# Batch 0's prologue: the third q pair transposed ahead of the second, the copies in that order, one dummy matmul taken out

## The chip, the cores and the metric

The kernel runs on one core of one Trainium2 chip. The metric is the device time of one execution in microseconds (us), as a median over runs. A profiled execution has its own span, counted from the first instruction of the program; it is some 2 us shorter than the timed value. The engines are PE (TensorE; "PEld" is its weight load), DVE (VectorE), ACT (ScalarE), POOL (GpSimd) and SP, which only issues DMAs here.

## The reference, cut to what matters

```python
q_s = softmax(q, axis=-1)            # 8 batches, 8 heads, 576 rows, 64 columns
k_s = softmax(k, axis=2)
kv  = einsum('bhsd,bhse->bhde', k_s, v)
x   = einsum('bhsd,bhde->bhse', q_s, kv)      # then to (4608, 512)
h   = x @ w_in                                # (512, 2048)
out = (h * sigmoid(beta * h)) @ w_out         # (2048, 512)
```

Nearly all the work is in the two products at the end. The attention of batch 0 is the prologue: nothing of the large products can start before it.

## The kernel before

Heads go in four pairs per batch. For each pair of batch 0, q is exponentiated (ACT), summed and scaled (DVE or POOL), transposed by PE into PSUM, and copied to SBUF. For each pair, PE also forms kv from exp(k) and v, and DVE scales the result. A matmul of the two gives x.

```python
def tpe(b, j, tag):          # four 128x128 transposes of pair j (PE)
    ...
def q_ev(b, j, eng):         # copy of the transposed pair to SBUF
    evac(eng, qsT[b][:, :, j, :], tp_of.pop((b, j))[:])
def kvz_mm(b, j, ...):       # kv group j: 18 small matmuls from exp(k) and the cast v
    ...
def kvz_norm(b, j, ...):     # DVE: one reciprocal, two multiplies
    ...
def warm(n, tag):            # n dummy matmuls 128x128x512 on zeros
    ...
```

The order written in the program is the order on each engine. The stretch around the change, and what comes a little later:

```python
q_mul(0, 2, 4, eng=G)        # pair 2 scaled on POOL
kz_exp(0, 0)
q_mul(0, 1, 4)               # pair 1 scaled on DVE
warm(10, tag="acc2")
beta_pe("acc0")
tpe(0, 3, "acc1")
tpe(0, 1, "acc2")
q_ev(0, 3, V)
tpe(0, 2, "acc3")
kz_exp(0, 1)
beta_ev()
q_ev(0, 1, V)
q_ev(0, 2, V)
vz_cast(0, 0, G)             # v of pair 0 cast on POOL
warm(1, tag="b0")
kz_exp(0, 2)
kvz_mm(0, 0, "b3", 1)
# ... three more kv groups, x of the four pairs, h(0,0) to h(0,3) ...
hpe(0, 7, [0], "b2")         # first product, block of columns 7, quarter 0 of w_in
th_act(0, 2)
hpe(0, 7, [1])
hpe(0, 4, [2])               # needs quarter 2 of w_in block 1
# ... then the second product of batch 0, mm_b(0, 0) to mm_b(0, 11) ...
kvz_mm(1, 0, "b1", 1)        # kv group of batch 1's first pair
tpe(1, 3, "b3")
```

The softmax here doesn't subtract the row's maximum and nothing guards it: scores larger than these inputs give would overflow.

Of the kernel before, what the change touches and what calls it, by code (L numbers as in the profile page):

```python
# [17 lines left out]
def kernel(  # L18
# [151 lines left out]
    def evac(eng, dst, src):  # L170
        if eng is nc.scalar:
            eng.copy(dst, src)  # L172
        else:
            eng.tensor_copy(dst, src)  # L174
# [8 lines left out]
    def kz_exp(b, j):  # L183
        if j == 0:
            ek_buf(b)
        nc.scalar.activation(ek[b][:, j, :], k_st[b][:, j, :], ACTF.Exp)  # L186
# [28 lines left out]
    def vz_cast(b, j, eng, m=1, part=None):  # L215
        r = slice(0, RW) if part is None else (slice(0, 5), slice(5, RW))[part]
        evac(
            eng,
            va[b][:, j : j + m, r, 0:D],
            v_st[b][:, j : j + m, :].rearrange("p j (i d) -> p j i d", i=RW)[:, :, r, :],  # L220
        )
# [63 lines left out]
    def bank(tag):  # L285
        if tag not in turns:
            return tag
        turns[tag] += 1
        return (HB if tag == "h" else AB)[(turns[tag] - 1) % 2]
# [3 lines left out]
    def tpe(b, j, tag):  # L293
        if j == 0:
            qsT[b] = work.tile([P, R, HP, P], BF16, tag="qsT", bufs=2, name=f"qsT{b}")
        tp_of[b, j] = ps.tile([P, R, P], BF16, tag=bank(tag), bufs=1, name=f"tp{b}_{j}")
        for i in range(R):
            nc.tensor.transpose(  # L298
                tp_of[b, j][:, i, :],
                eq[b][:].rearrange("p i (j x) d -> p i j (x d)", j=HP)[:, i, j, :],  # L300
                identity[:],
            )

    def q_ev(b, j, eng):
        evac(eng, qsT[b][:, :, j, :], tp_of.pop((b, j))[:])
# [222 lines left out]
    def warm(n, tag):  # L528
        t = ps.tile([P, 512], F32, tag=bank(tag), bufs=1, name=f"warm{warm_n[0]}")
        warm_n[0] += 1  # L530
        for _ in range(n):
            nc.tensor.matmul(t[:], xT[2][:, 0, 0:P], xT[2][:, 0, :])  # L532

    V, A, G = nc.vector, nc.scalar, nc.gpsimd
# [27 lines left out]
    def beta_pe(tag):  # L562
        tb = ps.tile([P, 512], F32, tag=bank(tag), bufs=1, name="tb")
        tb_of.append(tb)
        nc.tensor.transpose(tb[:, 0 : NJ // 2], beta_r[:, 0 : 2 * P : 2], ident8[:])
        nc.tensor.transpose(tb[:, NJ // 2 : NJ], beta_r[:, 1 : 2 * P : 2], ident8[:])

    def beta_ev():
        tb = tb_of[0]
        nc.scalar.copy(  # L570
            beta_t[:].rearrange("p (hh e) -> p e hh", e=2),
            tb[:, 0:NJ].rearrange("p (e hh) -> p e hh", e=2),
        )
# [62 lines left out]
    warm(10, tag="acc2")  # L636
    beta_pe("acc0")
    tpe(0, 3, "acc1")
    tpe(0, 1, "acc2")
    q_ev(0, 3, V)  # L640
    tpe(0, 2, "acc3")
    kz_exp(0, 1)
    beta_ev()
    q_ev(0, 1, V)
    q_ev(0, 2, V)
    vz_cast(0, 0, G)
    warm(1, tag="b0")
    kz_exp(0, 2)
    kvz_mm(0, 0, "b3", 1)
    vz_cast(0, 1, G)  # L650
# [340 lines left out]
```

## Time and profile before

| | value |
|---|---|
| time, median of the first three runs | 281.67 us (281.64 to 282.98) |
| profiled span | 279.8 us |
| PE busy | 272.2 us, 97% of the span |
| first kv matmul of batch 0 | 11.32 us |
| first reciprocal of the norms | 11.84 us |
| x of pair 2 | 13.94 us |
| h(0,4) with the late quarter of w_in (quarters 2 and 3 of block 1 come in one load) | 19.42 us |
| DMA rate from 9 to 36 us | 381 to 398 GB/s |

A PE that is busy 97% of the time tells that almost any saving elsewhere is hidden.

### The profile page before, as it was taken

The numbers are of one execution on the slowest core, as the hardware profiler recorded it, in microseconds if no ns is written. First come the engines' busy times: TensorE is split into PE (matmuls) and PEld (weight loads), VectorE is DVE, ScalarE is ACT, GpSimd is POOL, SyncE is SP. The second block draws the span as 40 slices with busy tenths as digits, with TensorE's granted clock in tenths as the row PEclk, the third lists the DMA queues.
The fourth block names the chain that finished last, engine by engine and source line by source line (L and its number), as shares of the span: only waits on it lengthen the run. The fifth ranks groups of instructions, "written<-read, shape, count | busy, mean of one in ns | idle before, by whom it ended". The sixth has DMA issues, their size and how long they took to land.

```text
span 279.8 us, 4448 instructions
## 1 busy us (share of the span) xinstructions
PE 272.2 (97%) x1712; PEld 128.0 (46%) x1739; DVE 174.9 (63%) x284; ACT 162.0 (58%) x247; POOL 40.5 (14%) x61
## 2 busy tenths in 40 slices
PE   8899999999999999999999999999999999999995
PEld 3444454444444444444444444444444544445444
DVE  3864786994478456944595549553864596354362
ACT  4757885947486447744684458444733574454451
POOL 1854227133030003000300021000000000000000
DMA  7999999999972991199318961641154034005004
GB/s 247 389 394 392 386 389 318 331 284 177 319 248 38 251 297 70 64 236 291 112 76 183 270 188 75 133 94 81 69 89 140 0 152 75 0 0 152 0 0 150
DMA packets 55316, 50.09 MB, mean 179 GB/s; under 512 B 26616, under 2 KB 47488, under 8 KB 55296
## 3 DMA queue, kind: packets, MB, share of 16 engines
q1 hardware_dynamic: 54368, 48.97, 60.2%
q10 hardware_dynamic: 928, 0.85, 0.9%
q8 instruction: 13, 0.21, 0.3%
q14 instruction: 7, 0.06, 0.1%
HBM read 36.71 MB, written 9.44 MB: 165 GB/s over the span
## 4 chain that ended last, share of the span: by engine, by line
PE 94%; DMA 3%; issue 1%; DVE 1%; ACT 1%; SPq 0%
PE h L404 45%; PE acc L453 43%; DMA k_st<-in_k_dram 3%; PE kv L342 2%; PE x L373 1%; PE acc L445 1%; PE kv L317 1%; PE x L389 1%; PE tp L298 1%; DVE kvp L332 0%; ACT ek L186 0%; DVE rk L329 0%; SPq L109 0%; ACT o L172 0%; PE x L364 0%
## 5 line engine op out<-in xcount | busy, mean ns | idle before, releaser
L418 DVE SCALAR_TENSOR_TENSOR g<-th,h 128x512 bf16<-128x512 bf16 x144 | 96.0, 681 | 79.4 <-ACT th L414 79.2
L414 ACT ACTIVATE th<-h,beta_t 128x512 bf16<-128x512 f32 x144 | 97.7, 686 | 81.9 <-PE h L404 81.3
L404 PE MATMUL h<-xT,w_in_b 128*128 128x512 bf16 x566 | 142.3, 379 | 0.8
L453 PE MATMUL acc<-w_out_b,g 128*128 128x512 bf16 x543 | 137.8, 379 | 1.5 <-issue 1.3
L404 PEld LDWEIGHTS <-w_in_b 128*128 128x128 bf16 x576 | 55.9, 98 | 66.3 <-ACT w_in_b L172 0.4
L453 PEld LDWEIGHTS <-g 128*128 128x128 bf16 x560 | 53.8, 98 | 66.0 <-issue 2.5
L174 POOL CAST va<-v_st 128x320 bf16<-128x320 f32 (+2 forms) x14 | 16.6, 1191 | 108.9 <-DMA v_st<-in_v_dram 108.9
L262 DVE TENSOR_REDUCE rq<-eq 128x16 f32<-128x1024 bf16 (+1 forms) x20 | 22.1, 1105 | 5.6 <-ACT eq L251 5.1
L268 DVE TENSOR_TENSOR eq<-eq,rq 128x1024 bf16<-128x1024 bf16 (+1 forms) x18 | 22.1, 1227 | 0.1
L172 ACT CAST xT<-x 128x512 bf16<-128x512 f32 x18 | 9.9, 588 | 17.0 <-PE x L373 14.9
L251 ACT ACTIVATE eq<-q_st 128x1024 bf16<-128x1024 f32 (+1 forms) x18 | 16.9, 955 | 3.4 <-DMA q_st<-in_q_dram 3.4
L174 DVE COPY o<-acc 128x512 f32<-128x512 f32 (+2 forms) x20 | 12.6, 641 | 3.6 <-PE acc L453 3.4
L172 ACT COPY o<-acc 128x512 f32<-128x512 f32 (+1 forms) x18 | 9.5, 570 | 8.5 <-PE acc L453 4.6
L174 DVE CAST xT<-x 128x512 bf16<-128x512 f32 x18 | 11.5, 682 | 2.6 <-PE x L373 1.8
L193 ACT ACTIVATE ek<-k_st 128x1024 bf16<-128x1024 f32 x12 | 12.6, 1050 | 0.0
L532 PE MATMUL warm<-xT 128*128 128x512 bf16 x25 | 8.0, 482 | 1.2 <-DVE xT L613 1.2
L174 POOL CAST w_in_b<-w_in 128x512 bf16<-128x512 f32 (+1 forms) x10 | 6.5, 656 | 5.7 <-DMA w_in<-in_moe_w_in_dram 5.5
L174 POOL CAST w_out_b<-w_out 128x1024 bf16<-128x1024 f32 x5 | 5.2, 1040 | 6.5 <-DMA w_out<-in_moe_w_out_dram 6.5
L186 ACT ACTIVATE ek<-k_st 128x576 bf16<-128x576 f32 x8 | 5.2, 679 | 1.0 <-DMA k_st<-in_k_dram 0.9
L263 DVE RECIPROCAL rq<-rq 128x16 f32<-128x16 f32 (+1 forms) x20 | 4.9, 243 | 0.7
L342 PEld LDWEIGHTS <-ek 128*64 128x64 bf16 x192 | 4.1, 111 | 2.5 <-issue 2.5
L532 PEld LDWEIGHTS <-xT 128*128 128x128 bf16 x25 | 2.9, 120 | 5.1 <-issue 2.8
(49 smaller groups left out, 84.7 us busy)
## 6 DMA issues: line engine op xcount, KB each, us to landing
out_dram<-o SPq DMA_DIRECT2D x14, 512.0 KB, 3.2
q_st<-in_q_dram SPq DMA_DIRECT2D x25, 256.0 KB, 4.1
k_st<-in_k_dram SPq DMA_DIRECT2D x6, 1024.0 KB, 9.6
v_st<-in_v_dram SPq DMA_DIRECT2D x6, 1024.0 KB, 11.1
w_in<-in_moe_w_in_dram SPq DMA_DIRECT2D x6, 512.0 KB, 9.9
v_st<-in_v_dram SPq DMA_DIRECT2D x8, 288.0 KB, 7.9
w_out<-in_moe_w_out_dram SPq DMA_DIRECT2D x4, 512.0 KB, 8.9
w_out<-in_moe_w_out_dram SPq DMA_DIRECT2D x2, 1024.0 KB, 10.5
```

The lines of the kernel that those rows point to most:

```text
L172: eng.copy(dst, src)
L174: eng.tensor_copy(dst, src)
L193: nc.scalar.activation(ek[b][:, :, h, :].rearrange("p i h d -> p h i d"), k_st[b][:, h, 0 : R * D].rearrange("p h (i d) -> p h i d", i=R), ...
L251: nc.scalar.activation(eq[b][:, :, s * m : (s + 1) * m, :].rearrange("p i h d -> p h i d"), q_st[b][:, s * m : (s + 1) * m, :].rearrange(" ...
L262: nc.vector.tensor_reduce(rq[b][:, 0, :, h], eq[b][:, :, h, :], axis=AX.X, op=ALU.add)
L268: eng.tensor_tensor(eq[b][:, :, h, :], eq[b][:, :, h, :], rq[b][:, 1, :, h].unsqueeze(3).to_broadcast((P, R, m, D)), ALU.mult,)
L342: nc.tensor.matmul(t[r * D : (r + 1) * D, j, :], ek[b][:, i, hd, :] if i < R else ekt[(b // 2) % 2][:, ds(hd * D, D)], va[b][:, i, hd, :] ...
L404: nc.tensor.matmul(h[:], w_unit(j, kt), x_of(c)[:, kt, :], start=(kt == 0), stop=(kt == KT - 1),)
L414: nc.scalar.activation(th[:], h_of[c, j][:], ACTF.Tanh, scale=beta_t[:, j : j + 1])
L418: nc.vector.scalar_tensor_tensor(out=g[:], in0=th_of.pop((c, j))[:], scalar=1.0, in1=h_of[c, j][:], op0=ALU.add, op1=ALU.mult)
L453: nc.tensor.matmul(acc[st][:], g[:, ds(st * P, P)], w_out_b[:, j, :], start=(j == 0), stop=(j == NJ - 1),)
L532: nc.tensor.matmul(t[:], xT[2][:, 0, 0:P], xT[2][:, 0, :])
```

## The change

Pair 2's scaled q is ready on POOL 0.55 us before pair 1's on DVE. The change lets PE transpose pair 2 first, in time in which it stood idle, makes DVE copy in the same order, and takes out the one dummy matmul ahead of the first kv group.

```diff
     beta_pe("acc0")
     tpe(0, 3, "acc1")
+    tpe(0, 2, "acc3")
+    q_ev(0, 3, V)
     tpe(0, 1, "acc2")
-    q_ev(0, 3, V)
-    tpe(0, 2, "acc3")
     kz_exp(0, 1)
     beta_ev()
+    q_ev(0, 2, V)
     q_ev(0, 1, V)
-    q_ev(0, 2, V)
     vz_cast(0, 0, G)
-    warm(1, tag="b0")
     kz_exp(0, 2)
     kvz_mm(0, 0, "b3", 1)
```

## The prediction

> **What bounds the kernel now.** I read the busy table of the page first, then the chain of waits over the first 15 us (the only stretch that the change touches), then each engine in order of time from 8.5 to 19.6 us, and last the waits of PE from 19.5 us on.
>
> ```profile
> PE 272.2 (97%) x1712; PEld 128.0 (46%) x1739; DVE 174.9 (63%) x284; ACT 162.0 (58%) x247; POOL 40.5 (14%) x61
> ```
>
> PE is busy 272.2 of 279.8 us, so the kernel is one long stream of matmuls and a change of order pays only where PE stands still. That is mostly in the prologue. The chain of waits, restricted to 9 to 12.2 us (start, length, what):
>
> ```profile
> 9.11 1.26 ACT ek L186 x2
> 10.37 0.07 ACT beta_t L570
> 10.44 0.13 issue
> 10.56 0.61 PE tp L298 x8
> 11.17 0.21 PE warm L532
> 11.39 0.43 PE kv L317 x18
> 11.81 0.02 issue
> 11.84 0.18 DVE rk L329
> ```
>
> The eight transposes (pairs 1 and 2), the dummy matmul and kv group 0 lie one after another on the path to the first reciprocal at 11.84. The wait before 10.56 is put down to the copy of beta. By the order of the program the first transpose of pair 1 cannot wait for that copy, which comes later; what it needs is pair 1's scaled q, and that multiply on DVE ends at the same moment (9.28 + 1.14 = 10.42). From 11.84 the chain is DVE alone: four norms of 0.69 us each (reciprocal plus two multiplies: rk at 11.84, 12.53, 13.22, 13.91), then x and the h matmuls. DVE and POOL in order of time:
>
> ```profile
> 9.28 1.14 DVE L268 TENSOR_TENSOR eq<-eq,rq 128x512 bf16<-128x512 bf16 x1
> 10.34 0.41 DVE L174 COPY qsT<-tp 128x512 bf16<-128x512 bf16 x1
> 10.99 0.75 DVE L174 COPY qsT<-tp 128x512 bf16<-128x512 bf16 x2 [0.23 <-PE tp L298]
> ...
> 8.82 1.05 POOL L268 TENSOR_TENSOR eq<-eq,rq 128x512 bf16<-128x512 bf16 x1
> 9.87 1.07 POOL L174 CAST va<-v_st 128x576 bf16<-128x576 f32 x1
> ```
>
> POOL finishes pair 2's scaled q at 9.87, 0.55 us ahead of pair 1's: today pair 1 is transposed first and pair 2 waits behind it. POOL then casts the first v group until 10.94, and kv group 0 cannot start before that.
>
> The decisive view is a few us later, everything in order of time from 18.6 to 19.6:
>
> ```profile
> 18.74 0.62 ACT L172 CAST w_in_b<-w_in 128x512 bf16<-128x512 f32 x1
> 18.77 0.61 POOL L174 CAST w_in_b<-w_in 128x512 bf16<-128x512 f32 x1 [1.40 <-DMA w_in<-in_moe_w_in_dram]
> 18.91 0.10 PEld L404 LDWEIGHTS <-w_in_b 128*128 128x128 bf16 x1 [0.28 <-issue]
> 19.27 0.68 ACT L414 ACTIVATE th<-h,beta_t 128x512 bf16<-128x512 f32 x1
> 19.41 0.11 PEld L404 LDWEIGHTS <-w_in_b 128*128 128x128 bf16 x2 [0.41 <-ACT w_in_b L172]
> ```
>
> POOL has been idle 1.40 us for the second half of w_in block 1 and starts when it lands, about 18.72; ACT casts its quarter in the same moment, until 19.36; the weight load of h(0,4) with that quarter starts at 19.41. So the matmul stream is pinned here by a landing, not by what came before. It hardly shows today: the matmul ahead starts at 19.12, 0.216 is one matmul, so PE would have gone on at 19.34 and loses only 0.08 us. From 19.5 to 39 the table of waits has no wait of PE: after 19.41 the order is simply worked off.
>
> **What the Trainium skill says.**
> - "TensorE: Matmul & The Clock Gate", Part 1: the array runs at half clock until it was busy about 3.4 us, and goes back after about that long an idle window. The trace agrees with the first: the dummies start 0.427 us apart until 5.43 and 0.216 us apart from then on. The longest gap of PE after that is 0.61 us, so taking the dummy away should not lower the clock.
> - The same page, Part 4, gives a PE transpose about 275 ns in a kernel. Here one takes 218 ns (median of 16) and starts follow each other by 0.055 us; I use these.
> - "GPSIMD Engine Reference", section 1, says that GpSimd shares its SBUF interfaces with VectorE, with contention when DVE has two SBUF inputs. The trace agrees: DVE's multiply beside POOL took 1.14 us against 0.69 alone, and the 128x576 cast 1.07 us in that overlap against 0.67 for the next.
> - "Perfetto Trace Analysis", Roofline, puts one core's ceiling at about 435 GB/s, that of its 16 DMA engines. Here DMA moves 387 to 398 GB/s from 9 to 36 us and the share of its engines is at 1.02 or above: the queue is full, and a landing time there follows from bytes, not from compute.
>
> **The change part by part.** The program after has two PE rows fewer (weight load and matmul of the dummy); the other engines have the same rows, DVE with copies 2 and 1 swapped. No DMA moves.
>
> (a) Pair 2's transposes first. PE ends pair 3's at about 9.96; pair 2 is scaled at 9.87, so its four go at about 10.0 and are done by 10.4, in what is idle time today. Pair 1's still start at 10.56 (DVE multiply) and end at 10.95. Four transposes x 0.055 = 0.22 us leave PE's path.
>
> (b) No dummy. The first kv matmul starts 0.31 us after the dummy's start (11.01 to 11.32). Without (a) the dummy costs about 0.2 us.
>
> (a) and (b) together would let kv group 0 start at about 10.9 (last transpose starts 10.73, plus some 0.15 by today's hand-overs). But the v cast ends at 10.94, so I take 11.00: **0.32 us** earlier than 11.32, not 0.42.
>
> (c) The copies. The copy of pair 3 stays at 10.34; copy 2 follows at 10.68 (back to back, 0.34 apart as today's last two), copy 1 at 11.02 to 11.43. kv group 0, 0.50 us from first start to last end, ends at 11.50; the reciprocal starts at about 11.53 instead of 11.84. DVE is free by then. **0.31 us** earlier.
>
> (d) The norms still take 0.69 us each, so the fourth starts at 13.60. kv groups 1, 2 and 3 wait for casts that do not move (ending 11.56, 11.95, 12.59), which lets group 3 end at about 13.2, still ahead of its norm. x of pair 2 goes at 13.62 instead of 13.94, and the h stream starts 0.31 us earlier. Its first weights, landing one after another and cast by 13.44, 14.10, 14.78 and 15.46, are there early enough.
>
> (e) At h(0,4)'s third matmul PE arrives at about 19.03 instead of 19.34 and waits until 19.41 all the same. The 0.08 us wait becomes about 0.39 us. **Sum at the end of the kernel: 0.31 won, 0.31 lost again, 0.0 us.**
>
> **The rivals.**
> 1. The gain survives: the w_in quarter could come earlier too. For it: an ACT that is 0.3 us ahead is free before the landing. Against: POOL, free for 1.40 us, could not start before 18.77 either, and the loads of that stretch are issued without waiting for anything that the change speeds up. If I am wrong here, 281.35 us (281.67 - 0.31).
> 2. The path is not shortened at all: the v cast or the contention of the earlier copies with POOL's casts holds kv group 0, or DVE's copies become the wait. For it: the cast ends only 0.38 us before today's kv start. Against: it is done at 10.94. The end would be the same 281.67, so the time cannot tell this from my theory; only the trace can.
> 3. Slower: without the dummy PE's clock falls back. A half-clock window of 3.4 us would cost some 1.7 us (estimate from the page on TensorE named above). Against: gaps of under 1 us, and the wait at 19.4 stays under 0.5 us. I give it a few per cent at most.
>
> **Range and chances.** The runs before are 281.64, 281.67 and 282.98. I predict **281.65 us**: no change, with a breath of the 0.08 us stall's jitter. The low end, 281.3, takes in rival 1; the high end, 282.1, takes in a median pushed by one of the longer executions. 2% would be 5.6 us, eighteen times all that is in play: faster 0.01, same 0.98, slower 0.01.
>
> **What the profile after would show.** Right: pair 2's transposes at about 10.0; first kv matmul near 11.0; first reciprocal near 11.5; x of pair 2 near 13.6; the POOL cast of w_in block 1 still at 18.77 with its long wait, and the weight load behind ACT's cast at 19.41 after a longer wait (about 0.3 us more in the matmul starts); from there the same times as before. Wrong: the load at 19.41 moved earlier (rival 1), the reciprocal still near 11.8 (rival 2), or matmuls 0.43 us apart after 9 us (rival 3). A shift of the landings themselves, which I take as fixed, would also break it.

## The result, and the profile after

The kernel after takes 281.93 us (median of six, 281.72 to 282.38), the kernel before 281.72 us in the runs set against it (281.61 to 282.98). The ratio is 1.0003, with a 95% interval of 0.9983 to 1.0022: the same. A ratio here is the mean of one kernel's fast runs over the mean of the other's in the same rounds, so it is not quite the ratio of the medians. The 0.2 us between the medians lie inside the interval, and nothing more is made of them. The interval is also too wide to choose between the prediction and its rival 1: 281.35 us would be 0.9987 of 281.72 and lies inside it. The choice rests on the traces.

First the prologue of the kernel after. DVE, POOL and PE in order of time from 9.3 to 12 us; the columns are start, length, engine, line and operation, output from input, and how many were merged:

```profile
9.43 1.15 DVE L268 TENSOR_TENSOR eq<-eq,rq 128x512 bf16<-128x512 bf16 x1
10.49 1.07 DVE L174 COPY qsT<-tp 128x512 bf16<-128x512 bf16 x3
11.66 0.17 DVE L329 RECIPROCAL rk<-kv 128x1 f32<-128x1 f32 x1
...
10.04 2.07 POOL L174 CAST va<-v_st 128x576 bf16<-128x576 f32 x3
...
9.70 1.32 PE L298 MATMUL tp<-identity,eq 128*128 128x128 bf16 x12
11.15 1.03 PE L317 MATMUL kv<-va,ek 64*64 64x65 bf16 x33
```

The page merges all twelve transposes in one row; their single records start at 9.70 us (pair 3), 10.08 us (pair 2) and 10.63 us (pair 1), so pair 2 now goes while DVE still scales pair 1. The three copies run back to back, and the first reciprocal is at 11.66 instead of 11.84. In this execution the loads landed about 0.14 us later than in the profile of before (k at 9.23 instead of 9.09 us), so against the landing of k the reciprocal is 0.32 us earlier: 11.659 - 9.230 = 2.43 us after it, where it was 11.836 - 9.089 = 2.75.

Then the place that the prediction called decisive. Everything in order of time from 18.6 to 19.7 us, the kernel after; the bracket gives the idle time ahead of an instruction and what ended it:

```profile
18.86 0.62 ACT L172 CAST w_in_b<-w_in 128x512 bf16<-128x512 f32 x1 [0.34 <-DMA w_in<-in_moe_w_in_dram]
18.89 0.62 POOL L174 CAST w_in_b<-w_in 128x512 bf16<-128x512 f32 x1 [1.36 <-DMA w_in<-in_moe_w_in_dram]
...
19.53 0.11 PEld L404 LDWEIGHTS <-w_in_b 128*128 128x128 bf16 x2 [0.70 <-ACT w_in_b L172]
19.53 0.39 PE L404 MATMUL h<-xT,w_in_b 128*128 128x512 bf16 x1 [0.21 <-ACT w_in_b L172]
```

ACT, which came straight from other work before, now waits 0.34 us for the landing as well, and PE for ACT's cast. The two matmuls on either side start 0.591 us apart. A matmul takes 0.216, so 0.375 us are lost, where it was 0.297 - 0.216 = 0.08. The chain of waits of the kernel after, from 9 us on, says it in another way:

```profile
2.65 8.08 DMA v_st<-in_v_dram
10.74 0.02 issue
10.75 8.08 DMA w_in<-in_moe_w_in_dram
18.83 0.02 issue
18.86 0.63 ACT w_in_b L172
19.48 0.04 issue
19.53 2.33 PE h L404 x10
```

In the kernel before this chain went through the prologue: exp of k, transposes, dummy, kv, norms, x. None of those is left in it. The prologue became shorter than the loads, and the path to the end now runs through the DMA: a load of v lands at 10.73 us, the second half of w_in block 1 is issued behind it at 10.75 and lands at 18.83.

A second place was not in the prediction. POOL and PE in order of time near 39 us, kernel before, then kernel after:

```profile
38.49 0.93 POOL L174 CAST va<-v_st 128x320 bf16<-128x320 f32 x1 [2.09 <-DMA v_st<-in_v_dram]
...
39.47 0.48 PE L317 MATMUL kv<-va,ek 64*64 64x65 bf16 x18
```

```profile
38.59 0.95 POOL L174 CAST va<-v_st 128x320 bf16<-128x320 f32 x1 [2.07 <-DMA v_st<-in_v_dram]
...
39.59 0.48 PE L317 MATMUL kv<-va,ek 64*64 64x65 bf16 x18
```

The kv group of batch 1's first pair starts 0.05 us after a cast of v that has itself waited over 2 us for its load. A full matmul and the first kv matmul behind it are at best 0.309 us apart in these traces; here it is 0.387 and 0.390, so each kernel waits 0.08 us. This is a second pin in the same stream (a place where the matmuls wait for a load), and both kernels end 240.34 to 240.36 us after it.

So the time can be cut into three stretches: from the landing of k to x of pair 2 (the prologue), from there to the kv group (1,0) (the stretch that waits for loads), and from there to the end. These are read from single records of the traces, and used below for all runs:

| run | k landed | prologue | to kv (1,0) | to the end |
|---|---|---|---|---|
| before | 9.09 | 4.85 | 25.54 | 240.36 |
| after | 9.23 | 4.53 | 25.83 | 240.34 |

The prologue is 0.32 us shorter and the next stretch 0.30 us longer.

The landing of k is not the best mark to measure from. What holds the prologue are the multiplies of pairs 1 and 2 and the cast of v behind one of them, and these follow q's second load, issued on ACT; k landed 3.01 to 3.04 us after it in ten of the 13 profiles, but 3.19 us in that of run 3. From the landing of that q load to x of pair 2 it is 7.88 to 7.89 us in all five profiles with the old order and the dummy (before and runs 5, 7, 9, 11) and 7.55 to 7.56 us in all six with the whole change (after and runs 3, 4, 6, 8, 10). So the 0.33 us are far above the scatter between executions.

### The profile page after: what moved, and what is told of

Same layout as the page of the kernel before. It is cut to its first block, busy times and chain, and to the rows that moved or that the text cites. A ratio compares the mean times of both kernels' runs of the same rounds, so it can differ in the third digit from the quotient of the medians.

```text
span 279.9 us, 4472 instructions
## 1 busy us (share of the span) xinstructions
PE 274.4 (98%) x1738; PEld 128.0 (46%) x1738; DVE 174.4 (62%) x284; ACT 162.1 (58%) x247; POOL 40.7 (15%) x61
## 4 chain that ended last, share of the span: by engine, by line
PE 92%; DMA 6%; SPq 1%; ACT 0%; issue 0%
PE acc L453 44%; PE h L404 43%; DMA v_st<-in_v_dram 3%; DMA w_in<-in_moe_w_in_dram 3%; PE kv L342 2%; PE x L373 1%; PE acc L445 1%; PE kv L317 1%; PE tp L298 0%; PE x L389 0%; ACT w_in_b L172 0%; SPq L578 0%; SPq L132 0%; SPq L109 0%; SPq L135 0%
## 5 line engine op out<-in xcount | busy, mean ns | idle before, releaser
L453 PE MATMUL acc<-w_out_b,g 128*128 128x512 bf16 x560 | 141.0, 379 | 0.0
L532 PE MATMUL warm<-xT 128*128 128x512 bf16 x24 | 7.3, 466 | 1.2 <-DVE xT L613 1.2
L354 DVE RECIPROCAL rk<-kv 128x4 f32<-128x4 f32 x6 | 1.1, 182 | 6.5 <-PE kv L342 6.5
```

The lines of the kernel that those rows point to most:

```text
L453: nc.tensor.matmul(acc[st][:], g[:, ds(st * P, P)], w_out_b[:, j, :], start=(j == 0), stop=(j == NJ - 1),)
L532: nc.tensor.matmul(t[:], xT[2][:, 0, 0:P], xT[2][:, 0, :])
```

## The experiments

The theory: the prologue's gain is real, and two late loads take it back, one at 19.4 us and one at 39.5 us. The rivals: the gain comes from another part of the change than thought; one load alone holds the kernel; an engine's queue between 20 and 39 us takes it; the landing could be moved. Eleven kernels were run, in three groups that each shared a chip and the runs of the kernel before. In some a wrong result is intended: they read other data, so that a wait is not needed, while every load and cast stays.

**1. The order alone.** The kernel after with the dummy put back:

```diff
+    warm(1, tag="b0")
     kz_exp(0, 2)
     kvz_mm(0, 0, "b3", 1)
```

> The new order of transposes and copies, with the dummy put back. My theory (the v cast on POOL is what kv group 0 waits for once the order is changed; the dummy alone is worth only some hundredths): last transpose starts 0.055 x 3 = 0.17 us after the multiply of pair 1 lets it go, the dummy 0.055 later, kv group 0 0.31 after the dummy, so within 0.05 us of the end of the first v cast plus 0.05, and the first reciprocal within 0.08 us of the kernel after, measured from the landing of k. Rival (the dummy is the part that pays): kv group 0 starts 0.2 us or more later than in the kernel after. Both: the weight load of h(0,4) still waits for the cast of the late quarter of w_in, and the end is the same, span about 279.8 to 280.0.

```profile
9.88 0.94 PE L298 MATMUL tp<-identity,eq 128*128 128x128 bf16 x12
10.66 0.38 PE L532 MATMUL warm<-xT 128*128 128x512 bf16 x1
10.96 1.21 PE L317 MATMUL kv<-va,ek 64*64 64x65 bf16 x39
...
11.48 0.17 DVE L329 RECIPROCAL rk<-kv 128x1 f32<-128x1 f32 x1
```

One run: 281.53 us, span 279.8. The dummy stands in front of the kv group and costs next to nothing: the prologue takes 4.51 us from k, as in the kernel after (from the q load 7.59 us, 0.03 more). The first v cast ends at 10.89, and the kv group starts 0.08 us later. The order carries nearly the whole gain of the prologue. The wait at h(0,4) is there (19.33 us, starts 0.560 apart).

**2. The dummy alone.** The kernel before without its one dummy.

> The kernel before with the dummy taken out and nothing else. My theory: the eight transposes still run one after another behind the multiply of pair 1 (last one starts 0.39 us after the first), kv group 0 starts about 0.15 us after the last transpose, 11.10 instead of 11.32, but DVE's third copy ends at the same time as before, so the first reciprocal is at 11.75 or later (DVE-bound), a gain of at most 0.1 us of the 0.31. Rival (the dummy pays): the reciprocal 0.2 us earlier, at about 11.62. Both: the end unchanged, because of the wait at h(0,4).

```profile
10.72 0.61 PE L298 MATMUL tp<-identity,eq 128*128 128x128 bf16 x8 [0.78 <-DVE eq L268]
11.26 0.93 PE L317 MATMUL kv<-va,ek 64*64 64x65 bf16 x33
...
11.14 0.76 DVE L174 COPY qsT<-tp 128x512 bf16<-128x512 bf16 x2 [0.23 <-PE tp L298]
11.81 0.16 DVE L329 RECIPROCAL rk<-kv 128x1 f32<-128x1 f32 x1
```

One run: 281.51 us, span 279.7. The prologue takes 4.68 us (from the q load 7.70): 0.16 of the 0.32 us, more than the 0.1 that was expected. The expected figure took the end of the last copy for the moment at which DVE is free, but the reciprocal starts at 11.81, 0.09 us ahead of the copies' end at 11.90. The two parts are not a sum: each takes PE's work from in front of the same kv group, and with the order changed taking out the dummy saves next to nothing. The first line also shows what releases pair 1's transposes: the multiply on DVE, and not the copy of beta that the profile of before named. One expectation failed: there is no wait at h(0,4) in this profile, because the late load landed 9.40 us after k, where it was 9.63 in the kernel before.

**3. The first late load not needed.** The kernel after, where h(0,4) to h(0,7) read block 0's weights for quarters 2 and 3 (wrong result):

```diff
-                w_unit(j, kt),
+                w_unit(j - 4 if c == 0 and j in range(4, 8) and kt >= 2 else j, kt),
```

> The kernel after, with the first batch's h(0,4) to h(0,7) reading block 0's weights for their last two quarters, so that they do not need the quarter of w_in that lands late (wrong result on purpose; all loads and casts stay). My theory: the wait of 0.37 us at h(0,4) is gone and the first matmul of the second product starts at about 21.3 instead of 21.70, 0.39 us earlier; but the gain meets a second landing, v of batch 1's first pair, at kv group (1,0) near 39.5, which still starts 0.05 us after that cast, so that the wait there grows from about 0.08 to about 0.47 us and the end moves by less than 0.05 us. Rival (one landing alone holds the kernel): the end 0.39 us earlier, span about 279.5.

```profile
21.11 1.24 PE L453 MATMUL acc<-w_out_b,g 128*128 128x512 bf16 x5
...
39.21 0.48 PE L317 MATMUL kv<-va,ek 64*64 64x65 bf16 x18 [0.23 <-POOL va L174]
...
38.38 0.78 POOL L174 CAST va<-v_st 128x320 bf16<-128x320 f32 x1 [2.30 <-DMA v_st<-in_v_dram]
```

One run: 281.36 us, span 279.6. The wait at h(0,4) is gone and the second product starts at 21.11 instead of 21.70. Then the kv group (1,0) waits for POOL's cast: starts 0.608 us apart, so 0.30 us are lost where it was 0.08. The second pin took 0.22 of the 0.375 us that the first gave up. The end came 0.35 us earlier than in the kernel after, where less than 0.05 was expected; by this number alone the rival (0.39 us) looks right. But the q load landed 0.24 us earlier in this execution (5.96 us, not 6.21). Measured from it the end is 0.11 us earlier and the kv group 0.14, with a cast of v that took 0.78 instead of 0.95 us. The group still starts 0.05 us after that cast, so the second load does hold it; how much it takes is known from this one execution only.

**4 and 5. Both late loads not needed**, on the kernel after and on the kernel before. In addition to the edit of run 3 (wrong result):

```diff
-                    va[b][r, j, i, :],
+                    va[0 if (b, j) == (1, 0) else b][r, j, i, :],
```

> As the run before it, and kv group (1,0) reads the v of batch 0 instead of its own (wrong result on purpose), so that it waits for no late cast. My theory: both waits gone, the stream from 40 us on about 0.37 + 0.08 = 0.45 us earlier than in the kernel after, span about 279.45 us, timed about 281.3. Rival (a third thing, DVE's multiply of pair 3 or g(0,12), holds PE near 39 to 40 us): a wait of 0.1 to 0.4 us appears there and the span is 279.6 or more.

> The kernel before with the same two waits taken away (wrong result on purpose). My theory: it gains only its own two waits, 0.08 at h(0,4) and 0.08 at kv group (1,0), span about 279.65; so the change itself is worth about 0.3 us here, the 0.31 us of the prologue, where it is worth nothing in the kernel as it is. Rival (the prologue's gain was never real, or is lost elsewhere): no difference between this one and the kernel after with the same two waits away.

Timed, they give 281.51 us (ratio to before 0.9992, 0.9969 to 1.0015; 281.3 was expected) and 281.43 us (0.9986, 0.9974 to 0.9998), which does not tell them apart; they also ran in different groups. The edit of the kernel after takes 4.54 us for the prologue and 25.36 to kv (1,0). That is 0.47 us less than the kernel after needs, close to the 0.45 expected. The edit of the kernel before met another late load in its profile, the last quarter of block 0. POOL, then PE:

```profile
16.56 0.62 POOL L174 CAST w_in_b<-w_in 128x512 bf16<-128x512 f32 x1 [1.43 <-DMA w_in<-in_moe_w_in_dram]
...
17.23 3.14 PE L404 MATMUL h<-xT,w_in_b 128*128 128x512 bf16 x13 [0.36 <-POOL w_in_b L174]
```

This cast starts at 14.85 us in the kernel before and here at 16.56, and PE loses 0.53 us to it (starts 0.744 apart). The packet records of the trace have one packet of that stretch, 2,048 bytes from 14.60 us on, that took 1.55 us, where the median is 0.08. The pair is inconclusive for the value of the change, so a cleaner pair follows as runs 8 and 9.

**6 and 7. Fewer dummies**, 3 in place of 10 ahead of the beta transposes, on the kernel after and on the kernel before. The question was why the late quarter lands so late: it lands 2.57 us after the quarter pair ahead of it (16.15 to 18.72 us), while the loads after it come 1.3 us apart. In the profile of before, a packet of the instruction queue runs in this stretch. The DMA view from 14.8 to 16.15 us of that kernel shows packets, MB and the share of the time of 16 engines:

```profile
q1 hardware_dynamic: 267, 0.51, 103.6%
q8 instruction: 1, 0.02, 4.8%
```

One packet took 4.8% of 16 x 1.35 us, which is 1.04 us of one DMA engine.

> The kernel after with 3 dummies instead of 10 ahead of the beta transposes: 14 PE rows fewer. Theory on why the quarter of w_in lands late: a 16 KB packet of the instruction queue, which starts when PE is at about row 266 (15.9 to 16.1 us), holds one DMA engine for about 1.04 us in front of that load's last packets. With 14 rows fewer it should come 7 matmuls x 0.216 = 1.5 us later, near 17.5 us, behind the load; the quarter then lands at about 17.5 instead of 18.8 us and the wait at h(0,4) goes away. Rival 1 (the landing follows from the bytes alone): it lands at 18.7 to 18.9 as before. Rival 2 (the dummies keep the clock up): matmuls 0.43 us apart after the gap from about 7.3 to 9.3 us, and the kernel 1 to 2 us slower.

> The same cut of 7 dummies on the kernel before. If the packet's place is set by PE's row count, the quarter lands early here too and the wait at h(0,4) goes away; but the kernel before comes to that place 0.3 us later, so the stream behind it should be about 0.3 us later than in the kernel after with few dummies, unless kv group (1,0) near 39.5 us still waits for its v in both. Rival: landing unchanged at 18.7.

The theory on the packet's place fell. From the profile of run 6, PE and POOL in order of time, then the same DMA view (14.8 to 16.24 us):

```profile
9.18 0.25 PE L565 MATMUL tb<-ident,beta_r 8*128 8x8 f32 x1 [1.39 <-DMA beta_r<-in_moe_beta_dram]
...
18.81 0.62 POOL L174 CAST w_in_b<-w_in 128x512 bf16<-128x512 f32 x1 [1.34 <-DMA w_in<-in_moe_w_in_dram]
```

```profile
q1 hardware_dynamic: 282, 0.54, 102.8%
q8 instruction: 1, 0.02, 4.8%
```

With 14 PE rows fewer the packet is at 15.89 us (15.88 in the kernel before, 16.06 in the kernel after, by the packet records of the traces) and the quarter lands at 18.75; in run 7 they are at 15.73 and 18.76. Rival 2 fell as well: PE idles 1.39 us ahead of the beta transposes, 0.216 us between matmuls stays, and the times are 281.77 us (ratio 0.9996, 0.9983 to 1.0009) and 281.98 us (1.0006, 0.9991 to 1.0021). Seven of the ten dummies do nothing for the time that these runs can see.

**8 and 9. No late load needed between 15 and 40 us**, on both kernels (wrong result):

```diff
-                w_unit(j, kt),
+                w_unit(j - 4 if c == 0 and j in range(4, 8) else j, kt),
-                w_out_b[:, j, :],
+                xT[2][:, 0, :] if c == 0 and j < 4 else w_out_b[:, j, :],
-                    va[b][r, j, i, :],
+                    va[0 if (b, j) == (1, 0) else b][r, j, i, :],
```

> The kernel after with every wait for a late load taken away between 15 and 40 us: h(0,4) to h(0,7) read block 0's weights only, the first 16 matmuls of the second product read a tile of zeros in place of w_out, kv group (1,0) reads batch 0's v (wrong result on purpose; all loads and casts stay). In the two runs with only some of the waits away the first half of w_in block 1 landed 0.6 and 1.5 us late and hid the answer. My theory: PE runs through, no start-to-start gap over 0.31 us between 19 and 40 us except the wait for DVE at h(0,7), and the group (1,0) starts about 0.5 us earlier against the landing of k than in the kernel after, whose end follows 240.36 us later. Beside the same edit on the kernel before it ends 0.3 us earlier (0.1 %), measured from the landing of k.

> The same edit on the kernel before. My theory: it runs through as well, but its kv group (1,0) comes 0.3 us later after the landing of k than in the edit of the kernel after, so the whole prologue gain of 0.31 us arrives at the end once no load is waited for. Rival (something other than the loads takes the gain, ACT's or DVE's queue between 20 and 39 us): the two differ by less than 0.1 us.

The start of the exp of k, which follows its landing, and of kv (1,0), in the edit of the kernel after and then in that of the kernel before:

```profile
9.16 1.26 ACT L186 ACTIVATE ek<-k_st 128x576 bf16<-128x576 f32 x2 [0.88 <-DMA k_st<-in_k_dram]
...
39.04 0.48 PE L317 MATMUL kv<-va,ek 64*64 64x65 bf16 x18
```

```profile
9.32 1.26 ACT L186 ACTIVATE ek<-k_st 128x576 bf16<-128x576 f32 x2 [0.88 <-DMA k_st<-in_k_dram]
...
39.53 0.48 PE L317 MATMUL kv<-va,ek 64*64 64x65 bf16 x18
```

From one to the other it is 29.88 us in the first and 30.21 in the second, 0.33 us apart. From x of pair 2 to kv (1,0) both take 25.36 us: with no load to wait for, the stretch no longer depends on the prologue, and the prologue's 0.33 us pass on to this group in full. Timed: 281.18 us (281.10 to 281.67; ratio to before 0.9980, 0.9968 to 0.9993) and 281.40 us (281.32 to 281.80; 0.9987, 0.9975 to 1.0000). The medians are 0.22 us apart, and so are the fastest runs, but the ranges overlap: that the gain arrives is shown by the traces, and the clock only agrees.

**10 and 11. Other work in the place of the waits**, a correct kernel. h(0,6) goes to a free PSUM bank and partly ahead of the late quarter; batch 1's first k and v loads go ahead of half a w_out load, with its cast moved down. Run 10 builds on the kernel after; run 11 is the same with the change under study undone. The core of the edit:

```diff
+    hpe(0, 6, [0], "acc3")
+    hpe(0, 6, [1])
     hpe(0, 7, [0], "b2")
     th_act(0, 2)
     hpe(0, 7, [1])
+    hpe(0, 6, [2])
+    hpe(0, 6, [3])
+    th_act(0, 6)
     hpe(0, 4, [2])
     ...                        # the old places of h(0,6), its tanh and gate are gone
-    w_load("out", 3, 0)
     load_kv(k_st, k, 1, "k_st", [0])
     load_kv(v_st, v, 1, "v_st", [0])
+    w_load("out", 3, 0)
```

> A correct kernel built on the kernel after that gives PE other work where it waits for loads: h(0,6) goes to the free bank acc3 and its first two quarters ahead of h(0,7), its last two first behind the wait; batch 1's first k and v loads go ahead of the fourth w_out load's first half, and that cast goes later on ACT. Expected: the wait at the late w_in quarter shrinks from 0.38 to about 0.1 us and the one for DVE ahead of h(0,7) goes; the first matmul of the second product at about 21.3 us instead of 21.7; kv group (1,0) without a wait, near 39.1; span about 279.4, time about 281.3, some 0.4 us under both kernels. Rival (the w_out cast or DVE's multiply of batch 1 becomes the next wait): most of it lost at 21.3 or near 39.3 us, span 279.7 or more.

> The filled kernel with the change under study undone (pair 1's transposes and copy first, the dummy there). My theory: the prologue comes 0.31 us later, the wait at the late quarter of w_in is absent or nearly so, and its end is 0.2 to 0.3 us later than the filled kernel's; if the late quarter still holds both, less than 0.1 us.

POOL and PE in order of time, run 10 and then run 11:

```profile
19.20 0.62 POOL L174 CAST w_in_b<-w_in 128x512 bf16<-128x512 f32 x1 [1.70 <-DMA w_in<-in_moe_w_in_dram]
37.61 0.46 POOL L174 CAST va<-v_st 128x320 bf16<-128x320 f32 x1 [1.06 <-DMA v_st<-in_v_dram]
...
19.84 1.90 PE L404 MATMUL h<-xT,w_in_b 128*128 128x512 bf16 x8 [0.26 <-ACT w_in_b L172]
39.39 0.48 PE L317 MATMUL kv<-va,ek 64*64 64x65 bf16 x18
```

```profile
37.15 0.46 POOL L174 CAST va<-v_st 128x320 bf16<-128x320 f32 x1 [1.01 <-DMA v_st<-in_v_dram]
...
38.98 0.48 PE L317 MATMUL kv<-va,ek 64*64 64x65 bf16 x18
```

The v cast now ends over a microsecond ahead of kv (1,0), so the second pin is gone in both (0.309 us between starts). The first is not quite: in the profiled execution of run 10 the late quarter landed 0.3 us later than in the kernel after, and PE lost 0.42 us to it. So that one profile misses the 0.1 us expected: its second product starts at 21.59 us and kv (1,0) at 39.39, where 21.3 and 39.1 were expected. The profile of run 11 shows no wait there. Timed, run 10 takes 281.20 us (281.10 to 281.53; ratio 0.9980, 0.9967 to 0.9992), run 11 281.42 us (281.27 to 281.94; 0.9990, 0.9976 to 1.0003). Run 10 is the only correct kernel here whose interval lies clear of 1. It beats the kernel before by about 0.2%, and by its median the kernel after too, which ran in other rounds. The change under study is worth 0.22 us by the medians of runs 10 and 11, with overlapping ranges.

## Why the prediction was right

The median, 281.93 us, lies in the range of 281.3 to 282.1, if in its upper half, and the traces show the reason that was given for no change. Point by point:

- **(a) to (d), the prologue.** Against the landing of k, which was 0.14 us later, the first kv matmul came at 11.00 (11.00 predicted), the reciprocal at 11.52 (11.53) and x of pair 2 at 13.62 (13.62). Pair 1's transposes were released by DVE's multiply, as argued against the profile's attribution; run 2 shows it by name. Run 1 confirms that the v cast holds the kv group and that the dummy costs only 0.03 us once the order is changed. Run 2 puts the dummy without the new order at 0.19 us for the kv group's start and 0.16 us for the prologue, where 0.2 was said.
- **(e), the loss.** The wait at h(0,4) grew to 0.375 us (0.39 predicted), and POOL's cast started at 18.89 us, the old place plus 0.11 us of later landing.
- **Rival 1** (the quarter comes earlier too) is out: ACT was free 0.34 us before the landing. **Rival 2** (prologue not shortened) is out by the table of stretches. **Rival 3** (the clock falls) is out: after 9 us no two 512-column matmuls that follow each other in the kernel after start 0.40 to 0.46 us apart, and even a gap of 1.39 us in run 6 left the 0.216 us as they were. The page's row of the granted clock cannot tell this: it reads 9 tenths in the first slices too, where the dummies start 0.427 us apart until 4.88 us.
- **What it missed.** It said that the order is simply worked off after 19.41 us. It is, but only to 39.5 us, where a second late load, v of batch 1's first pair, would have taken part of the gain even if the first had not: in run 3 PE lost 0.30 us there instead of 0.08. So "no change" had some luck: with (e) wrong, part of the gain would have been lost all the same. With no late load to wait for the gain arrives: runs 8 and 9. It also gave the DMA rate as 387 to 398 GB/s up to 36 us; from 31 to 36 us it was 381, on which nothing rests.
- **A step that was too simple** is that a landing follows from bytes. The late quarter came 2.57 us after the one ahead, though 0.5 MB at 390 GB/s take about 1.3 us. The Trainium skill ("DMA: Bandwidth & Descriptors", Why a DMA increments its semaphore by 16 and not by 1) says that a DMA runs on up to 16 engines that finish independently and that only the full count means landed. The traces agree: the late load's semaphore has 16 updates, and in the kernel before 15 of them came by 17.49 us, about when the bytes ask, and the last at 18.72 (17.64 and 18.83 in the kernel after). So one engine was behind, not the whole queue. An instruction packet that holds one engine for 1.04 us would delay the whole landing by about that much. The same skill ("Runtime: NRT & Kernel Launch", Terms) says that instruction memory is refilled in blocks of 16 KiB, and the packet has 16,384 bytes. The sizes fit roughly (outside runs 4 and 5, the last update came 0.99 to 1.56 us after the fifteenth), but the traces do not say on which engine the packet was, and no run moved it, so this cause is argued and not shown. A rival stands in run 5: there an ordinary packet of 2,048 bytes took 1.55 us, and one update of block 0's last quarter came at 16.51 us, the other 15 by 14.69. What sets its time is open; run 6 shows that the number of PE rows ahead of it is not what does.

## What to carry to other kernels

Before counting a gain in a prologue, look downstream for the first instruction that waits for a load, and compare the idle time of an engine that had nothing else to do ahead of it: POOL's 1.40 us of waiting told that PE could not be let through earlier. Slack in the loads has to be made, or the waits filled with other work, before a shorter prologue is worth anything; then look for the next pin, because there may be one. When two runs differ by tenths of a microsecond, measure from a landing in each trace, since landings themselves moved by some 0.5 us from one execution to the next (k between 9.00 and 9.43 us, the late load between 18.62 and 19.15). Take the landing on which the path really starts: from q's load the prologues of one order agree within 0.01 us, from k's they are up to 0.18 us apart.

## What the Trainium skill lacked or had wrong

- "TensorE: Matmul & The Clock Gate", Part 4, gives about 275 ns for a transpose in a kernel and says that the full clock does not engage for transposes. Here they took 218 ns (median of 16) and started 0.055 to 0.056 us apart, which is the pace that its Part 1 gives for a warm array. Dummies had raised the clock before; whether transposes alone would, no run shows.
- "GPSIMD Engine Reference", section 1, names the contention with VectorE but no size for it, and no page has one for these instructions: a multiply on DVE took 1.14 us beside POOL and 0.69 alone.
- "DMA: Bandwidth & Descriptors" gives no time for a packet of instructions: one of 16,384 bytes took 1.04 to 1.10 us, at 15.5 to 16.3 us in every profile.
- No page has a time for the hand-over from a 512-column matmul to small tiled ones: 0.309 us between starts, where two full ones are 0.216 apart.
